# Attention first halves: softmax scaling moved from the probabilities to the product with v

## The chip, the cores and the metric

The kernel runs on one core of a Trainium2 chip as a single launch. The metric is the device time in microseconds (us). Where a profile is shown, it is one execution taken by the hardware profiler; its time axis counts from the span's start.

## The reference

Causal attention with a decay, then two feed-forward blocks. Shapes: 4 batches, 8 heads, 576 positions, head size 64; the rows of all batches form a 2304 x 512 matrix x. All in float32.

```
scores = q k^T / sqrt(D)
scores = where(causal, -1e9, scores + cum[i] - cum[j])      # cum: running sum of log f
attn   = exp(scores - rowmax)
attn   = attn / (rowsum(attn) + 1e-9)
x      = attn v                          # -> (B*S, H*D) = (2304, 512)
h = x w_in;  g = max(0.01 h, h);  x = g w_out               # first block, 512 -> 2048 -> 512
h = x w_in2; g = h * sigmoid(h);  out = g w_out2            # second block
```

## The kernel before

**Order of the work.** Each batch's 576 queries are cut in a first half (queries 0 to 255, which see 256 keys) and a second half (queries 256 to 575, which see up to 576 keys). The 64 pieces of work "head n" run in the order: n = 0 to 31 are the 8 heads of the first halves of batches 0 to 3, n = 32 to 63 those of the second halves. Two neighbouring heads make a pair, so the first halves are 16 pairs. The product x w_in of the first block (`hidden_part`, L992, tiles `hps` and `hpw`) starts as soon as the columns of x of batch 0's first half and the weights are there, and from then on it is TensorE's other work beside the attention, up to the stage where the attention has ended; the rest of the two blocks follows.

**The planner.** No engine's order is written by hand. `Plan` runs the program's generators at build time on planned costs (`act_cost`, `dve_cost`, `pe_cost` and constants in the code); each `op(engine, cost, fn, rank)` joins its engine's queue, and a lower rank goes first. Attention operations have rank 0, hidden products and the decoding of the weights rank 1. The order in which the plan issues them is the order of the instructions on each engine, and that order is fixed: an instruction that has to wait holds up all that stand behind it on its engine. A step's successor joins a queue a little after the step's planned end (`lat`), and an engine that is free at that moment takes the next operation that is ready. Until the first hidden unit is through, TensorE gets filler products (L477, L479) whenever its planned queue is empty.

**One head of a first half.** It has two blocks of 128 queries: block 0 sees 128 keys, block 1 sees 256.

1. `score`: TensorE makes the scores of a block (L775, tile `sps`), VectorE adds the mask, scales by -1/8 and takes the row minimum (L755, tile `sc`, minimum in a column of the small tile `st`), ScalarE takes the exponential and the row sums (L798).
2. `shares`: when both blocks have their exponentials, VectorE adds 1e-9 to the two sums (L817) and takes their reciprocals (L818).
3. Each block is multiplied in place by its reciprocals, on VectorE (L806) or ScalarE (L808), whichever the plan finds sooner done.
4. `transp`: TensorE transposes the three 128 x 128 pieces (L856, tile `tps`), and one copy brings them to SBUF (L372 on ScalarE or L373 on VectorE, tile `pf`).
5. `weigh`, once for a pair: TensorE multiplies v with the transposed probabilities (L925, tile `av`): the first head's 64 rows of the result go to partitions 0 to 63, the second head's to 64 to 127. Per head these are a product over 256 columns and one over 128.
6. `to_ring`: the result is split in a rounded high part (ScalarE, L372, tile `ring`) and a rest (VectorE, L387), from which the hidden product reads.

The second halves go the same way with three blocks per head. The tile `av` has one buffer (the pairs of batch 0 take turns with a second bank).

**Other work on ScalarE and VectorE in this stretch.** The weights come as 64-bit words and are decoded (L1777 on ScalarE, L1778, L1779, L1781 on VectorE, tiles `cy`, `ct`), then split (`w<-ct`, L372 and L387). A hidden product waits for the split weights it reads.

Of the kernel before, what the change touches and what calls it, by code (L numbers as in the profile page):

```python
# [9 lines left out]
F32 = mybir.dt.float32  # L10
# [3 lines left out]
ALU = mybir.AluOpType  # L14
# [6 lines left out]
G_BUFS = 3  # L21
GT_BUFS = 3
RING_BUFS = 8
WST_BUFS = 2
OUT_AT = 40
WY_BUFS = 3
# [75 lines left out]
class Plan:  # L102
# [90 lines left out]
    def wait(self, *names):  # L193
        def step(resume):
            missing = [n for n in names if n not in self.seen]
            if not missing:
                resume()
                return
            left = [len(missing)]

            def one():
                left[0] -= 1
                if not left[0]:
                    resume()

            for n in missing:
                self.waiting.setdefault(n, []).append(one)

        return step
# [8 lines left out]
    def signal(self, name):  # L218
        self.seen[name] = True
        for fn in self.waiting.pop(name, []):  # L220
            fn()

    def take(self, pool, bufs):


        def step(resume):
            i = self.taken[pool] = self.taken.get(pool, -1) + 1
            if i < bufs or (pool, i - bufs) in self.given:
                resume(i)
            else:  # L230
                self.queue[pool, i - bufs] = lambda: resume(i)

        return step

    def give(self, pool, i):
        self.given[pool, i] = True
        fn = self.queue.pop((pool, i), None)
        if fn:
            fn()
# [61 lines left out]
def fused_kernel(ctx, tc, qt, kt, va, vb, ft, w1, wi2, wo2, out):  # L301
# [430 lines left out]
    def score(n, i):  # L732
        half = head_info(n)[1]
        t0 = HALF[half][0]
        q0, qn, qk, kn = BLOCKS[half][i]
        kn = min(kn, q0 + qn)
        ht = heads[n]
        if half == 0 and i == 1:
            sc = ht["sc"][:, 256:512]
        else:  # L740
            ht["i_sc", i] = yield take("sc", SC_BUFS)
            ht["sc"] = sc = at["sc"].tile([128, S], F32, tag="sc", name="sc")
        if i == 0:
            ht["i_st"] = yield take("st", ST_BUFS)
            p.start(shares(n, stats[ht["i_st"] % ST_BUFS]))
        st = stats[ht["i_st"] % ST_BUFS]
        pieces = [(0, kn)] if kn <= 512 else [(0, kn // 2), (kn // 2, kn // 2)]
        done = []

        def least(a, ps, k0, w, bank):  # L750
            z0 = ZOFF - q0 + k0
            yield wait("zmask" if half else "zmask0")
            if a:
                yield wait(("min", n, i, a - 1))
            yield dve(w, lambda: nc.vector.tensor_tensor_reduce(  # L755
                out=sc[0:qn, k0:k0 + w], in0=ps[0:qn], in1=zmask[0:qn, z0:z0 + w], scale=-0.125,
                scalar=(MASK if a == 0 else st[0:qn, 2 * i + a - 1:2 * i + a]), op0=ALU.add, op1=ALU.min,
                accum_out=st[0:qn, 2 * i + a:2 * i + a + 1],
            ), 0)
            give(*bank)  # L760
            signal(("min", n, i, a))

        def product(ps, k0, w):
            qs = slice(q0 - t0, q0 - t0 + qn)
            if n < DIRECT:
                nc.tensor.matmul(ps[0:qn], ht["s1"][0:64, qs], ht["m1"][0:64, k0:k0 + w], start=True, stop=False)
                for c in range(w // 128):
                    nc.tensor.matmul(
                        ps[0:qn, 128 * c:w], opened["fs"][:, c, n:n + 1].broadcast_to([128, qn]),
                        opened["tri"][:, 0:w - 128 * c], start=False, stop=c == w // 128 - 1,  # L770
                    )
                return
            ops = (("s1", "m1"),) if plain(n) else (("s1", "m1"), ("s2", "m2"))
            for r, (x, y) in enumerate(ops):
                nc.tensor.matmul(  # L775
                    ps[0:qn], ht[x][:, qs], ht[y][:, k0:k0 + w], start=r == 0, stop=r == len(ops) - 1
                )

        for a, (k0, w) in enumerate(pieces):
            if n < H:  # L780
                bank = ("h", (yield take("h", 2)))
                ps = ps_h.tile([128, w], F32, tag="h", name="sps")
            else:
                bank = ("sp", (yield take("sp", 3)))
                ps = ps_at.tile([128, w], F32, tag="sp", name="sps")
            if n < DIRECT:
                yield wait("tri", ("logs", 0))
            cost = pe_cost(w, 4 if plain(n) else 2)
            if n < DIRECT:
                cost += sum(pe_cost(w - 128 * c, 4) for c in range(w // 128))  # L790
            yield op("pe", cost, lambda: product(ps, k0, w), 0, 0.05)
            p.start(least(a, ps, k0, w, bank))
        signal(("scored", n, i))
        if "i_qk" in ht and i == len(BLOCKS[half]) - 1:
            give("qk", ht["i_qk"])
        a = len(pieces) - 1
        yield wait(("min", n, i, a))
        yield act(kn, lambda: nc.scalar.activation(  # L798
            sc[0:qn, 0:kn], sc[0:qn, 0:kn], ACTF.Exp, scale=-1.0, bias=st[0:qn, 2 * i + a:2 * i + a + 1],
            accum_out=st[0:qn, 6 + i:7 + i],  # L800
        ), 0, 0.28)
        signal(("exp", n, i))
        yield wait(("shares", n))
        r = st[0:qn, 9 + i:10 + i]
        yield p.either([
            ("dve", dve_cost(kn, True) + 0.06, lambda: nc.vector.tensor_scalar(  # L806
                sc[0:qn, 0:kn], sc[0:qn, 0:kn], r, None, op0=ALU.mult), 0.0),
            ("act", act_cost(kn, 0.1), lambda: nc.scalar.mul(sc[0:qn, 0:kn], sc[0:qn, 0:kn], r), 0.0),  # L808
        ], 0, PE_LAT)
        ht["p"][i] = sc  # L810
        signal(("p", n, i))

    def shares(n, st):

        nb = len(BLOCKS[head_info(n)[1]])
        yield wait(*[("exp", n, i) for i in range(nb)])
        yield dve(1, lambda: nc.vector.tensor_scalar(st[:, 6:6 + nb], st[:, 6:6 + nb], 1e-9, None, op0=ALU.add), 0)  # L817
        yield dve(1, lambda: nc.vector.reciprocal(st[:, 9:9 + nb], st[:, 6:6 + nb]), 0)  # L818
        signal(("shares", n))
        yield wait(*[("p", n, i) for i in range(nb)])  # L820
        give("st", heads[n]["i_st"])

    def chunk_cols(half, c):

# [52 lines left out]
            p.start(rest(*w))  # L877

    def bank_for(n, tn):
        if n < H:  # L880
            name = ("av", ("acc", 0))[n // 2 % 2]
            i_av = yield take(name, 1)
            tag, pool_ = (("av", ps_at), ("acc0", ps_acc))[n // 2 % 2]
            return name, i_av, pool_.tile([128, tn], F32, tag=tag, name="av", bufs=1)
        i_av = yield take("av", 1)
        return "av", i_av, ps_at.tile([128, tn], F32, tag="av", name="av", bufs=1)
# [19 lines left out]
    def weigh(n):  # L906

        if n % 2 == 0:
            return
        _, half, _ = head_info(n)  # L910
        tn = HALF[half][1]
        both = [heads[n - 1], heads[n]]
        last = len(EDGES[half]) - 2
        chunks = range(last + 1)
        yield wait(("values", n // 2), *[("pt", m, c) for m in (n - 1, n) for c in chunks])
        v2, i_vh = pair_v.pop(n // 2)
        name, i_av, ps = yield from bank_for(n, tn)
        todo = [(c, [ht["pt"].pop(c) for ht in both]) for c in chunks]

        def product():  # L920
            for c, pts in todo:
                kw = EDGES[half][c + 1] - EDGES[half][c]
                _, lo = chunk_cols(half, c)
                for i, (pt, o, _) in enumerate(pts):
                    nc.tensor.matmul(  # L925
                        ps[64 * i:64 * i + 64, lo:tn], v2[0:kw, i, c], pt[0:kw, o:o + tn - lo],
                        start=c == 0, stop=c == last, skip_group_check=True,
                    )

        yield op("pe", 0.25 + sum(pe_cost(tn - chunk_cols(half, c)[1], 4) for c in chunks), product, 0, 0.05)  # L930
        for _, pts in todo:
            for _, _, i_pt in pts:
                for i in i_pt:
                    give("pt", i)
        if i_vh is not None:
            give("vh", i_vh)
        heads.pop(n - 1)
        heads.pop(n)
        yield from to_ring(n, ps, "a", "d")
        give(name, i_av)  # L940

    def x_ready(j, c=None):

# [1155 lines left out]
```

## Time and profile before

| | us |
|---|---|
| median of 3 runs | 946.62 (945.66 to 947.48) |
| profiled execution, its own time | 942.98 |
| its span | 941.3 |
| TensorE busy | 928.3 (99%) |
| VectorE busy | 749.0 (80%) |
| ScalarE busy | 597.9 (64%) |
| DMA | 208 GB/s mean |

Busy time counts an engine's instructions from their start to their end; TensorE's records overlap, since a product starts to stream before the one ahead has drained, so what one instruction costs is read from start to start. PE is TensorE's matmul row, PEld its weight loads, DVE is VectorE, ACT is ScalarE.

### The profile page before, as it was taken

The numbers are of one execution on the slowest core, as the hardware profiler recorded it, in microseconds if no ns is written. First come the engines' busy times: TensorE is split into PE (matmuls) and PEld (weight loads), VectorE is DVE, ScalarE is ACT, GpSimd is POOL, SyncE is SP. The second block draws the span as 40 slices with busy tenths as digits, with TensorE's granted clock in tenths as the row PEclk, the third lists the DMA queues.
The fourth block names the chain that finished last, engine by engine and source line by source line (L and its number), as shares of the span: only waits on it lengthen the run. The fifth ranks groups of instructions, "written<-read, shape, count | busy, mean of one in ns | idle before, by whom it ended". The sixth has DMA issues, their size and how long they took to land.

```text
span 941.3 us, 17621 instructions
## 1 busy us (share of the span) xinstructions
PE 928.3 (99%) x6287; PEld 877.3 (93%) x6287; DVE 749.0 (80%) x1769; ACT 597.9 (64%) x1320; POOL 54.5 (6%) x61
## 2 busy tenths in 40 slices
PE   9999999999999999999999999999999999999998
PEld 7888887788889989999999999999999999999998
DVE  6999966998998754889998699759554598888886
ACT  6899866676787763676545577556466764444442
POOL 2004302021121200000000000000000000000000
PEclk9999999999999999999999999999999999999999
DMA  7569344776676419995957685897747774544542
GB/s 201 152 176 308 120 128 152 250 235 226 217 250 189 141 57 314 347 363 181 326 214 234 170 266 171 290 336 251 271 169 245 238 239 116 154 116 139 147 120 90
DMA packets 157523, 195.42 MB, mean 208 GB/s; under 512 B 9222, under 2 KB 142966, under 8 KB 157404
## 3 DMA queue, kind: packets, MB, share of 16 engines
q1 hardware_dynamic: 157004, 193.91, 64.1%
q8 instruction: 49, 0.80, 0.4%
q10 hardware_dynamic: 432, 0.39, 0.1%
q14 instruction: 38, 0.31, 0.1%
HBM read 124.61 MB, written 69.65 MB: 206 GB/s over the span
## 4 chain that ended last, share of the span: by engine, by line
PE 71%; DVE 11%; DMA 10%; ACT 5%; issue 2%; SPq 1%; DVEq 0%; ACTq 0%
PE m L1590 19%; PE m L1732 18%; PE hpw L992 11%; PE acc L1283 8%; PE sps L775 4%; PE av L925 4%; PE tps L856 3%; DMA w<-w_d 3%; DMA g_d<-gw 2%; DMA gq<-g_d 2%; DVE sc L755 2%; PE hps L992 2%; DVE gs L387 2%; ACT sc L798 1%; DMA w_d<-f 1%
## 5 line engine op out<-in xcount | busy, mean ns | idle before, releaser
L1283 PE MATMUL acc<-gs,w 128*128 128x384 f32 x1008 | 181.5, 339 | 1.2 <-DVE gs L387 1.0
L992 PE MATMUL hpw<-ring,w 128*128 128x320 f32 (+1 forms) x960 | 179.7, 330 | 0.2 <-ACT gw L1104 0.2
L1590 PE MATMUL m<-xc,w 128*128 128x384 f32 x1008 | 179.8, 339 | 0.0
L1283 PEld LDWEIGHTS acc<-gs,w 128*128 128x128 f32 x1008 | 177.6, 188 | 2.2 <-DVE gs L387 1.6
L1732 PE MATMUL m<-w,gc 128*128 128x256 f32 x1512 | 178.6, 280 | 0.0
L1732 PEld LDWEIGHTS m<-w,gc 128*128 128x128 f32 x1512 | 178.4, 188 | 0.0
L1590 PEld LDWEIGHTS m<-xc,w 128*128 128x128 f32 x1008 | 177.7, 188 | 0.2
L992 PEld LDWEIGHTS hpw<-ring,w 128*128 128x128 f32 x960 | 149.8, 188 | 7.0 <-issue 0.5
L372 ACT CAST gc<-g 128x512 fp32r<-128x512 f32 (+1 forms) x180 | 80.4, 490 | 88.7 <-DVE g L1422 50.6
L798 ACT ACTIVATE sc<-sc,st 128x576 f32<-128x576 f32 (+2 forms) x160 | 93.0, 582 | 30.6 <-DVE st L755 29.1
L1216 ACT CAST gs<-gq 128x768 fp32r<-128x768 f32 x84 | 69.6, 835 | 47.5 <-PE acc L1283 26.1
L387 DVE TENSOR_TENSOR gs<-gq,gs 128x768 fp32r<-128x768 f32 x84 | 79.5, 952 | 18.0 <-ACT gs L1216 17.5
L387 DVE TENSOR_TENSOR gc<-g,gc 128x512 fp32r<-128x512 f32 (+1 forms) x180 | 89.8, 524 | 3.3 <-ACT gc L372 2.1
L755 DVE CUSTOM_DVE_ANT_0 sc<-sps,zmask 128x288 f32<-128x288 f32 (+2 forms) x160 | 71.4, 449 | 24.6 <-PE sps L775 16.0
L1422 DVE TENSOR_TENSOR g<-g 128x256 f32<-128x256 f32 x144 | 58.3, 418 | 18.6 <-DMA g<-g_d 18.0
L856 PE MATMUL tps<-ident,sc 66*107 66x66 f32 (+3 forms) x480 | 67.4, 269 | 1.4 <-DVE st L755 0.4
L775 PE MATMUL sps<-m,s 66*128 66x288 f32 (+5 forms) x256 | 64.1, 331 | 4.4 <-DVE st L755 2.7
L387 DVE TENSOR_TENSOR w<-w 128x512 fp32r<-128x512 f32 x84 | 56.0, 686 | 15.1 <-ACT w L1984 15.1
L1984 ACT CAST w<-w 128x512 fp32r<-128x512 f32 x84 | 50.9, 619 | 24.1 <-DMA w<-w_d 23.7
L383 POOL TENSOR_TENSOR m<-qk,m 64x288 fp32r<-64x288 f32 x46 | 49.4, 1095 | 266.5 <-ACT m L372 127.9
L856 PEld LDWEIGHTS tps<-ident,sc 66*107 66x107 f32 (+3 forms) x480 | 55.8, 151 | 7.1 <-issue 1.2
L992 PE MATMUL hps<-ring,w 128*128 128x256 f32 x384 | 58.7, 291 | 0.0
(125 smaller groups left out, 1129.1 us busy)
## 6 DMA issues: line engine op xcount, KB each, us to landing
w<-w_d SPq DMA_DIRECT2D x84, 256.0 KB
gq<-g_d SPq DMA_DIRECT2D x48, 384.0 KB
g_d<-z SPq DMA_DIRECT2D x24, 768.0 KB
g<-g_d SPq DMA_DIRECT2D x36, 512.0 KB
w_d<-f SPq DMA_DIRECT2D x16, 896.0 KB
g_d<-gw SPq DMA_DIRECT2D x32, 320.0 KB
qk<-in_kt_dram SPq DMA_DIRECT2D x32, 288.0 KB
wst<-in_w_dram SPq DMA_DIRECT2D x18, 512.0 KB
```

The lines of the kernel that those rows point to most:

```text
L372: ("act", act_cost(n, base), lambda: nc.scalar.copy(dst, src), 0.0),
L387: ("dve", dve_cost(n), lambda: nc.vector.tensor_tensor(dst, a, b, op=ALU.subtract), 0.0),
L755: yield dve(w, lambda: nc.vector.tensor_tensor_reduce(out=sc[0:qn, k0:k0 + w], in0=ps[0:qn], in1=zmask[0:qn, z0:z0 + w], scale=-0.125, sca ...
L775: nc.tensor.matmul(ps[0:qn], ht[x][:, qs], ht[y][:, k0:k0 + w], start=r == 0, stop=r == len(ops) - 1)
L798: yield act(kn, lambda: nc.scalar.activation(sc[0:qn, 0:kn], sc[0:qn, 0:kn], ACTF.Exp, scale=-1.0, bias=st[0:qn, 2 * i + a:2 * i + a + 1], ...
L856: nc.tensor.transpose(ps[0:k1 - k0, o:o + qn], ht["p"][i][0:qn, k0:k1], ident[0:qn, 0:qn])
L992: nc.tensor.matmul(dst, w[:, wi, c * 128:(c + 1) * 128], x(xi, c), start=(first_ and c == 0 and r == 0), stop=(c == KC - 1 and r == 2), sk ...
L1216: yield act(2 * TB, lambda: nc.scalar.copy(t[:, 0], src), 0, 0.09)
L1283: nc.tensor.matmul(dst, w[:, e, wi, j * 128:(j + 1) * 128], x[:, xi, e], start=start and s == 0 and e == 0 and r == 0, stop=stop and s == ...
L1422: ("dve", dve_cost(n), lambda: nc.vector.tensor_tensor(dst, a, b, op=op_), 0.0),
L1590: nc.tensor.matmul(dst, w[:, wi, c * 128:(c + 1) * 128], x[:, xi, c], start=start and c == 0 and r == 0, stop=stop and c == 1 and r == 2, ...
L1732: nc.tensor.matmul(banks[b][:, e], t[:, gi, a * 128:(a + 1) * 128], w[:, wi], start=begin and a == 0 and r == 0, stop=jp == NP // 2 - 1 an ...
```

## The change

It concerns the first halves alone (n = 0 to 31). Step 3 is dropped: the exponentials go to the transposes and to the product with v as they are. The small tile `st` is now shared by a pair: minima in columns 0 to 3, sums in 4 to 7, reciprocals in 8 to 11; step 2 runs once per pair (`pair_shares`), on four columns.

In `weigh` the pair's bank grows from 256 to 512 columns. Ahead of the product with v TensorE makes four products into the upper 256 columns (`spread`): for each block and each head a reciprocal column, repeated 64 times, is the 128 x 64 weight, and the 128 x 128 identity is streamed. The result holds, in the 64 partitions of each head, the reciprocal of each query in its column. One copy (`factors`, on ScalarE or VectorE) brings these 256 columns to SBUF, in a new tile `xn` with two buffers; after the product with v, VectorE multiplies the product by them into the same tile, which frees the bank, and `to_ring` reads `xn` instead of the bank.

```
         signal(("exp", n, i))
+        if not half:
+            yield p.after(PE_LAT - LAT)
+            ht["p"][i] = sc
+            signal(("p", n, i))
+            return
         yield wait(("shares", n))
...
+    def pair_shares(n, st):
+        yield wait(*[("exp", m, i) for m in (n, n + 1) for i in range(2)])
+        yield dve(1, lambda: nc.vector.tensor_scalar(st[:, 4:8], st[:, 4:8], 1e-9, None, op0=ALU.add), 0)
+        yield op("dve", dve_cost(1), lambda: nc.vector.reciprocal(st[:, 8:12], st[:, 4:8]), 0, PE_LAT)
+        signal(("shares", n))
...
     def bank_for(n, tn):
+        if head_info(n)[1] == 0:
+            tn = 2 * tn
...
-        yield wait(("values", n // 2), *[("pt", m, c) for m in (n - 1, n) for c in chunks])
+        yield wait(("values", n // 2), *([] if half else [("shares", n - 1)]), *[("pt", m, c) for m in (n - 1, n) for c in chunks])
...
+        def spread():
+            for i, (q0, qn, _, _) in enumerate(BLOCKS[0]):
+                for e in range(2):
+                    r = st[:, 8 + 2 * i + e:9 + 2 * i + e].broadcast_to([128, D])
+                    nc.tensor.matmul(
+                        ps[64 * e:64 * e + 64, tn + q0:tn + q0 + qn], r, ident, start=True, stop=True,
+                        skip_group_check=True,
+                    )
+        def factors():
+            yield copy(tn, x, ps[:, tn:2 * tn], "ad", 0, None, 0.125, False)
+        if not half:
+            i_x = yield take("xn", XN_BUFS)
+            x = at["const"].tile([128, tn], F32, tag="xn", name="xn", bufs=XN_BUFS)
+            yield op("pe", 0.5, spread, 0, 0.05)
+            give("st", i_st)
+            p.start(factors(), lambda: signal(("factors", n)))
...
-        yield from to_ring(n, ps, "a", "d")
+        if half:
+            yield from to_ring(n, ps, "a", "d")
+            give(name, i_av)
+            return
+        yield wait(("factors", n))
+        yield op("dve", 0.42, lambda: nc.vector.tensor_tensor(x, ps[:, 0:tn], x, op=ALU.mult), 0)
         give(name, i_av)
+        yield from to_ring(n, x, "a", "d")
+        give("xn", i_x)
```

## Rows read from the trace of the kernel before

**Rows 1.** Busy us (instructions) of PE, PEld, DVE, ACT, POOL by stretch; granted clock; DMA.

```profile
12.00:33.00 21.00, 21.00 (x167) 18.07 (x165) 20.33 (x97) 18.36 (x62) 0.00 (x0) 1.00 0.68 183
33.00:80.00 47.00, 46.62 (x360) 38.85 (x359) 46.10 (x198) 44.01 (x144) 2.72 (x2) 1.00 0.69 203
80.00:120.00 40.00, 36.70 (x287) 33.03 (x286) 39.36 (x105) 35.10 (x83) 16.41 (x14) 1.00 0.54 172
120.00:941.30 821.30, 812.82 (x5433) 778.87 (x5432) 639.89 (x1352) 494.74 (x1021) 30.31 (x30) 1.00 0.65 211
```

**Rows 2.** Timeline, TensorE, 32 to 38 us: start, duration, instruction and count.

```profile
32.77 0.60 PE L775 MATMUL sps<-k,s 65*128 65x256 f32 x2
33.20 0.49 PE L856 MATMUL tps<-ident,sc 128*128 128x128 f32 x3
33.62 0.87 PE L925 MATMUL av<-pf,v 128*64 128x256 f32 x8
...
34.67 0.60 PE L992 MATMUL hps<-ring,w 128*128 128x256 f32 x3
...
37.69 0.87 PE L925 MATMUL av<-pf,v 128*64 128x256 f32 x8
```

**Rows 3.** Groups by form, TensorE, 33 to 80 us: busy, mean ns, idle before.

```profile
L992 PE MATMUL hps<-ring,w 128*128 128x256 f32 x132 | 23.5, 305 | 0.0
```

**Rows 4.** Timeline, TensorE's dense stretch: 60 hidden records and the next start.

```profile
127.19 7.36 PE L992 MATMUL hps<-ring,w 128*128 128x256 f32 x60
134.39 2.23 PE L992 MATMUL hpw<-ring,w 128*128 128x512 f32 x9
```

**Rows 5.** Waits of TensorE, 80 to 120 us: us in total, times, longest.

```profile
PE sps L775 <- DVE st L755: 1.4, 2, 0.8
```

**Rows 6.** Timeline, TensorE around one pair's product with v.

```profile
59.33 0.60 PE L775 MATMUL sps<-k,s 65*128 65x256 f32 x2
59.85 0.87 PE L925 MATMUL av<-pf,v 128*64 128x256 f32 x8
60.65 0.49 PE L775 MATMUL sps<-k,s 65*128 65x128 f32 x2
```

**Rows 7.** Timeline, TensorE's weight loads around the same product (idle before, releaser).

```profile
59.85 0.63 PEld L925 LDWEIGHTS av<-pf,v 128*64 128x64 f32 x8 [0.33 <-issue]
60.65 0.30 PEld L775 LDWEIGHTS sps<-k,s 65*128 65x128 f32 x2 [0.17 <-DVE st L818]
```

**Rows 8.** Groups by form, 0 to 95 us: fillers, scalings, the shares' two steps.

```profile
L479 PE MATMUL fps<-zmask 128*128 128x128 f32 x60 | 10.3, 274 | 0.0
...
L806 DVE TENSOR_SCALAR sc<-sc,st 128x256 f32<-128x256 f32 x23 | 8.0, 346 | 0.0
...
L808 ACT ACTIVATE sc<-sc,st 128x128 f32<-128x128 f32 x14 | 5.5, 393 | 0.2 <-DVE st L818 0.2
L817 DVE TENSOR_SCALAR st<-st 128x2 f32<-128x2 f32 x32 | 5.2, 162 | 0.6 <-ACT sc L798 0.5
L818 DVE RECIPROCAL st<-st 128x2 f32<-128x2 f32 x32 | 5.1, 158 | 0.0
L806 DVE TENSOR_SCALAR sc<-sc,st 128x128 f32<-128x128 f32 x18 | 5.0, 280 | 0.0
...
L808 ACT ACTIVATE sc<-sc,st 128x256 f32<-128x256 f32 x9 | 4.5, 499 | 0.0
```

**Rows 9.** Timeline, VectorE, 30 to 33 us.

```profile
30.44 0.16 DVE L818 RECIPROCAL st<-st 128x2 f32<-128x2 f32 x1
30.52 0.40 DVE L387 TENSOR_TENSOR ring<-av,ring 128x256 fp32r<-128x256 f32 x1
...
30.84 0.54 DVE L806 TENSOR_SCALAR sc<-sc,st 128x128 f32<-128x128 f32 x2
...
31.29 0.16 DVE L817 TENSOR_SCALAR st<-st 128x2 f32<-128x2 f32 x1
...
32.51 0.69 DVE L387 TENSOR_TENSOR w<-ct,w 128x512 fp32r<-128x512 f32 x1
```

More of the change, by code (lines that the diff above doesn't have):

```diff
@@ L23 @@
 RING_BUFS = 8
+XN_BUFS = 2
 WST_BUFS = 2
@@ L743, in score @@
         if i == 0:
-            ht["i_st"] = yield take("st", ST_BUFS)
-            p.start(shares(n, stats[ht["i_st"] % ST_BUFS]))
+            if half or n % 2 == 0:
+                ht["i_st"] = yield take("st", ST_BUFS)
+                p.start((shares if half else pair_shares)(n, stats[ht["i_st"] % ST_BUFS]))
+            else:
+                ht["i_st"] = heads[n - 1]["i_st"]
         st = stats[ht["i_st"] % ST_BUFS]
+        col = (lambda a: 2 * i + a) if half else (lambda a: 2 * i + n % 2)
+        total = 6 + i if half else 4 + 2 * i + n % 2
         pieces = [(0, kn)] if kn <= 512 else [(0, kn // 2), (kn // 2, kn // 2)]
@@ L756, in least @@
                 out=sc[0:qn, k0:k0 + w], in0=ps[0:qn], in1=zmask[0:qn, z0:z0 + w], scale=-0.125,
-                scalar=(MASK if a == 0 else st[0:qn, 2 * i + a - 1:2 * i + a]), op0=ALU.add, op1=ALU.min,
-                accum_out=st[0:qn, 2 * i + a:2 * i + a + 1],
+                scalar=(MASK if a == 0 else st[0:qn, col(a - 1):col(a - 1) + 1]), op0=ALU.add, op1=ALU.min,
+                accum_out=st[0:qn, col(a):col(a) + 1],
             ), 0)
@@ L798, in score @@
         yield act(kn, lambda: nc.scalar.activation(
-            sc[0:qn, 0:kn], sc[0:qn, 0:kn], ACTF.Exp, scale=-1.0, bias=st[0:qn, 2 * i + a:2 * i + a + 1],
-            accum_out=st[0:qn, 6 + i:7 + i],
+            sc[0:qn, 0:kn], sc[0:qn, 0:kn], ACTF.Exp, scale=-1.0, bias=st[0:qn, col(a):col(a) + 1],
+            accum_out=st[0:qn, total:total + 1],
         ), 0, 0.28)
         signal(("exp", n, i))
+        if not half:
[3 more added lines that the diff above has]
+            return
         yield wait(("shares", n))
@@ L918, in weigh @@
         todo = [(c, [ht["pt"].pop(c) for ht in both]) for c in chunks]
+        i_st = both[0].get("i_st")
+        st = stats[i_st % ST_BUFS]
+        def spread():
[14 more added lines that the diff above has]
+            p.start(factors(), lambda: signal(("factors", n)))
         def product():
@@ L928, in product @@
                     )
-        yield op("pe", 0.25 + sum(pe_cost(tn - chunk_cols(half, c)[1], 4) for c in chunks), product, 0, 0.05)
+        yield op("pe", 0.25 + sum(pe_cost(tn - chunk_cols(half, c)[1], 4) for c in chunks),
+                 product, 0, 0.05)
         for _, pts in todo:
```

## The prediction

> **What bounds the kernel now.** I read the busy times by stretch first. The reader is to see that TensorE is at work all the time at a granted clock of 1.00 (2.4 GHz): it is idle for 0.4 us between 33 and 80, for 3.3 us between 80 and 120, and for 8.5 us in the 821 us behind that [rows 1]. In the two stretches from 12 to 80 VectorE is busy 97 and 98%, ScalarE 87 and 94%; from 120 on they have room (78 and 60%) [rows 1]. The first halves, which the change touches, begin in the first of these stretches and end early in the third, and there three engines are full together. So the question is which of them sets the pace there.
>
> A busy TensorE can hide small gaps, so I looked at what fills it. Between 33 and 80 it does 132 records of the hidden product with no idle time ahead of them [rows 3]. In a dense stretch 60 such records take from 127.19 to 134.39, 0.12 us each [rows 4], so they are 15.8 of the 47 us, and they are work that waits for its turn: the plan never ran out of it. What the attention takes more of TensorE there pushes hidden work back by the same amount, and since TensorE is idle for no more than 8.5 us of the 821 that follow, what is pushed back comes out at the end. What the attention takes less of VectorE and ScalarE brings nothing by itself in that stretch; it can only bring something at the two places where TensorE has no real work or waits.
>
> The first place is ahead of 34.67, where the first hidden product stands [rows 2]. Up to there TensorE's gaps hold 60 filler records [rows 8]. The hidden product needs split weights; the last step of the second weight stands in VectorE's order at 32.51, for 0.69 us [rows 9]. Then a pair's product with v goes first, at 33.62 [rows 2]. So this start hangs on VectorE, which is full. The second place is 80 to 120: the 3.3 us there [rows 1] are TensorE held up in its order by late VectorE results, the largest group of them scores that wait for a row minimum [rows 5].
>
> **The change, part by part.**
>
> *TensorE, added: four small products per pair.* Nothing like `spread` stands in the trace; the product with v is nearest, since it too has 64-column weights and two heads side by side. A score product over 256 columns takes from 32.77 to 33.20, 0.43 us [rows 2], so one over 128 columns takes 0.215. The product with v is two of 256 and two of 128 columns, 1.29 us one after the other; it takes from 59.85 to 60.65, 0.80 us [rows 6], so the two heads' products run side by side (0.645) with 0.155 us lost behind them. Ahead of it the score product that began at 59.33 lasts to 59.85, 0.52 us where 0.43 is usual [rows 2, 6], 0.09 more. Going into and out of this shape thus costs 0.245 us, which the idle time ahead of the weight loads also shows [rows 7]. The four products of `spread` are 4 x 128 columns in two columns of the array: 0.43 us side by side, 0.86 if they do not overlap. If they stood directly ahead of the product with v, they would share its way in and out: 0.43. But the product with v joins the queue 0.05 us after the planned end of `spread`, and TensorE, free at that moment, takes the next hidden piece, which is always ready. So I expect them apart, each with its own 0.245: 0.43 + 0.245 = 0.68 us. Bounds: 0.43 (adjacent) to 0.86 + 0.245 = 1.1 (no overlap). I take 0.68.
>
> The Trainium skill, page "TensorEngine Tiling (Array Packing)", section Key Properties, says that changing the tiling mode, not just the tile, drains TensorE. By that rule each `spread` that stands apart pays a drain of its own, which the idle times ahead of the loads bear out [rows 7]; the sum would be the one at 0.68, not the one at 0.43.
>
> Four of the 16 pairs have their product with v ahead of 34.67 (the fifth stands at 33.62 [rows 2] and belongs to the saturated part). Those four take the place of fillers: 4 x 0.68 = 2.7 us against 60 records of about half of 0.215, 6.5 us [rows 2, 8]; they cost nothing as long as these fillers are there, and 2.7 us if they were not. The other 12 cost 12 x 0.68 = **+8.2 us** (5.2 to 13).
>
> *VectorE and ScalarE, removed.* The 64 scalings: 41 on VectorE (23 of 256 and 18 of 128 columns), 23 on ScalarE [rows 8]. One of each form on VectorE take from 30.84 to 31.29 together, 0.45 us [rows 9]; split by their durations 0.25 and 0.20, this makes 23 x 0.25 + 18 x 0.20 = 9.4 us. On ScalarE 5.5 + 4.5 = 10.0 us at full durations [rows 8], some 8 with the overlap that VectorE's have. Of the 64 steps on sums 32 go; one takes from 30.44 to 30.52, 0.08 us to the next start [rows 9], so 2.6 us.
>
> *VectorE and ScalarE, added.* 16 products with the factors, a VectorE operation of 128 x 256 from PSUM, like the rest for the ring: 30.52 to 30.84, 0.32 us [rows 9], 5.1 us. 16 copies of the factors, same size, on either engine, some 5 us. Net relief: 9.4 + 8 + 2.6 - 5.1 - 5 = about 10 us over both, 5 each, of some 70 us in which they are full.
>
> *What the relief brings.* Ahead of the start, 5 of 16 pairs' worth: 10 x 5/16 = 3.1 us over two engines, 1.5 us on each. Against it stands the longer way of the last pair of batch 0: `spread`, a piece of other work, the product with the factors, some 1 us more, and the scaling and its hand-overs, about as long, less. The weights decide rather than that pair, so I take **-1.0 us** (0 to -3). In 80 to 120, VectorE has 3 or 4 us less behind it; of the 3.3 us of idle time there, and 0.4 before [rows 1], I take 70% back: **-2.6 us** (0 to -3.7).
>
> *Waits that are added.* `spread` waits for the pair's reciprocals; behind it on TensorE stand scores and hidden pieces. Between the last exponential and the product with v lie the transposes and a copy, longer than the two steps of 0.16 us [rows 8], so I cost this at nothing; were that cover gone, each 0.1 us late would cost 12 x 0.1 = 1.2 us. The product with the factors waits for the copy of them; behind it on VectorE stand row minima and copies of transposes. The product with v and a hidden piece, together over 1 us, cover the copy. The bank is held longer, about 3 us in place of 2; pairs follow each other by 37.69 - 33.62 = 4.1 us [rows 2], so I cost that at nothing, and 0.5 us a pair, 6 us, if it did not fit. No DMA is added or moved.
>
> *The sum.* 8.2 - 1.0 - 2.6 = +4.6 us. On the profiled execution's own 942.98 (1.7 around its span of 941.3) that is 947.6; the median of the runs shown stands 3.6 us above it, at 946.62, and on that the forecast is **951.2 us**.
>
> **The rivals.**
>
> *A, TensorE has room (faster).* Its weight loads are busy for 38.85 of 47 us between 33 and 80 [rows 1], so 8.2 us are without one. If the stretch is really paced by VectorE and ScalarE, the 12 x 0.68 fit into that room, and only the gains stand: -1.0 - 2.6 = -3.6, 943.0 us. It decides if less than 1.7 us of the 8.2 shows. Against it: the hidden records have no idle time ahead of them [rows 3], and a score record of 0.215 us streams longer than its load takes, so a share below one is no proof of room. The Trainium skill, page "Perfetto Trace Analysis", section Identifying the Most-Contended Engine, holds busy matmul time for a bad measure and weight-load busy time for a good one; by that rule TensorE stands at 83% there, VectorE at 98% is the bound, and this rival is right. Chance 0.16.
>
> *B, cheap and recovered (same).* `spread` costs 0.43, 5.2 us in all, and the gains reach their ends, -3.7 and -1.0: +0.5, 947.1 us. It needs the plan to set the two products together. Chance 0.18.
>
> *C, no overlap (slower, more).* The copies of one column as weights do not run side by side: 12 x 1.1 = 13.2, less 3.6: +9.6, 956.2 us. Chance 0.09.
>
> *D, a new wait (slower).* The bank or the factors come late: 4.6 + 6, about 957 us; or the plan, which is made anew with other costs, sets other waits behind 120, where 8.5 us of idle time [rows 1] can grow as well as shrink. Chance 0.06.
>
> **How the numbers follow.** The forecast, +2 to +8.5, has 0.51. A change within 0.2%, 1.9 us, is about what a measurement of this kernel can't tell from none. Slower: 0.51 + 0.09 + 0.06 = 0.66; same: B, 0.18; faster: A, 0.16. The range goes from A's 943.0 to 956.0, just under C, so that about 2 in 10 are outside; the forecast's own is 948.6 to 955.
>
> **What would show it.** In the profile after: 128 weight loads more of 64 columns, in groups of 8 that take 0.6 to 0.7 us to the next start and stand apart from the product with v; no scaling lines at the first halves; the first hidden record at 33 to 34.5; less TensorE idle time between 80 and 120; and the same record of the second stage (the dense stretch's end, say) some 4 to 5 us later. The forecast is wrong if hidden records get through as early as before despite `spread`, if the groups take under 0.45 us or over 0.9, or if idle time behind 120 changes by more than 3 us.

## The result, and the profile after

| | before | after |
|---|---|---|
| median of 7 runs each | 946.62 us (944.66 to 948.67) | 952.65 us (949.57 to 954.80) |
| ratio after / before | | 1.0075, 95% interval 1.0056 to 1.0094 |
| profiled execution, its span | 941.3 us | 949.9 us |

By the ratio the change makes the kernel 7.1 us slower (5.3 to 8.9); the two medians differ by 6.0. I had forecast 4.6 us slower. The changed kernel, run once more beside other experiments (e8), came out at 1.0089 (1.0074 to 1.0105). The profiled execution stands 8.6 us above that of before.

First the busy times by stretch of the changed kernel, columns as in [rows 1]:

```profile
12.00:33.00 21.00, 19.16 (x153) 15.04 (x151) 16.95 (x69) 16.67 (x56) 0.00 (x0) 1.00 0.57 154
33.00:80.00 47.00, 46.78 (x378) 35.33 (x374) 44.92 (x170) 39.79 (x130) 1.56 (x2) 1.00 0.72 210
80.00:120.00 40.00, 38.96 (x305) 34.45 (x304) 38.60 (x113) 35.67 (x86) 15.07 (x14) 1.00 0.56 175
120.00:949.90 829.90, 820.83 (x5500) 786.76 (x5498) 640.70 (x1353) 497.03 (x1023) 30.55 (x31) 1.00 0.64 209
```

The relief is there: between 12 and 80 VectorE is busy for 61.9 us in place of 66.4, ScalarE for 56.5 in place of 62.4 [rows 1]. TensorE's idle time between 80 and 120 fell from 3.3 us to 1.0, nearly as forecast. But behind 120 it is 9.1 in place of 8.5, and ahead of 33 there are 1.8 us that were not there before; 1.1 of them are a score product that waits for the load of the keys of a later head (in e8, the same kernel, the idle time ahead of 33 is 0.7). All four stretches together have 12.2 us of idle time before and 12.2 after. So idle time makes none of the 8.6 us. Where they come from stands in the records of the hidden product alone, here of the changed kernel (columns: PE, PEld, granted clock, DMA):

```profile
33.00:80.00 47.00, 10.56 (x57) 7.89 (x57) 1.00 0.72 210
80.00:120.00 40.00, 22.46 (x157) 20.27 (x156) 1.00 0.56 175
```

57 records got through between 33 and 80, where there were 132 [rows 3]. Another 9 ran ahead of 33, the first at 27.3, so by 80 there are 66 fewer. At the 0.12 us of a dense stretch [rows 4] that is 7.9 us of hidden work pushed back. The forecast's sign, a record of the second stage that starts 4 to 5 us later, came out larger too: the wide hidden records (tile `hpw`) start at 142.0 in place of 134.4 [rows 4], and the last of them at 418.7 in place of 409.3 (the last two times of such a line are the group's first and last start):

```profile
L1042 PE MATMUL hpw<-ring,w x960: 302/309/496, 142.0 to 418.7; 128*128 128x320 f32 x153, 128*128 128x512 f32 x39
```

What took the place shows in TensorE's timeline of one pair in the changed kernel:

```profile
38.61 0.60 PE L781 MATMUL sps<-k,s 65*128 65x256 f32 x2
39.14 0.66 PE L947 MATMUL av<-ident,st 128*64 128x128 f32 x8
39.73 0.49 PE L781 MATMUL sps<-k,s 65*128 65x128 f32 x2
40.05 0.49 PE L874 MATMUL tps<-ident,sc 128*128 128x128 f32 x3
40.48 0.87 PE L967 MATMUL av<-pf,v 128*64 128x256 f32 x8
41.28 0.70 PE L781 MATMUL sps<-k,s 65*128 65x256 f32 x2
```

The small products (L947) stand apart from the product with v (L967), as forecast. They take from 39.14 to 39.73, 0.59 us, the 0.43 side by side and 0.155 behind them that the working had. The score product ahead takes 0.53 us where 0.43 is usual, about the 0.09 of the way in that the working had as well. But the score product behind them also takes longer, from 39.73 to 40.05, 0.32 us, where the working had 0.215 for one of 128 columns: another 0.10, which the forecast did not count. The rows of before have it as well, behind a product with v:

```profile
60.65 0.49 PE L775 MATMUL sps<-k,s 65*128 65x128 f32 x2
60.90 0.60 PE L992 MATMUL hps<-ring,w 128*128 128x256 f32 x3
...
36.58 0.39 PE L775 MATMUL sps<-k,s 65*128 65x128 f32 x2
36.72 0.60 PE L992 MATMUL hps<-ring,w 128*128 128x256 f32 x3
```

The first score product stands right behind a product with v and takes 0.25 us to the next start, the second stands elsewhere and takes 0.14.

The groups by form of the changed kernel, 0 to 95 us (columns as in [rows 3]), show the rest:

```profile
L947 PE MATMUL av<-ident,st 128*64 128x128 f32 x128 | 10.5, 285 | 0.0
...
L987 DVE TENSOR_TENSOR xn<-av,xn 128x256 f32<-128x256 f32 x16 | 6.6, 410 | 0.5 <-ACT xn L373 0.5
...
L374 DVE COPY xn<-av 128x256 f32<-128x256 f32 x13 | 5.5, 425 | 2.7 <-PE av L967 2.1 <-PE av L947 0.5
L480 PE MATMUL fps<-zmask 128*128 128x128 f32 x24 | 4.2, 278 | 0.0
...
L373 ACT COPY xn<-av 128x256 f32<-128x256 f32 x3 | 1.1, 373 | 1.2 <-PE av L967 0.8 <-PE av L947 0.2
```

All 128 records of the small products; 13 of the 16 copies on VectorE, 3 on ScalarE; and 24 fillers where there were 60 [rows 8].

### The profile page after: what moved, and what is told of

Same layout as the page of the kernel before. It is cut to its first block, busy times and chain, and to the rows that moved or that the text cites. A ratio compares the mean times of both kernels' runs of the same rounds, so it can differ in the third digit from the quotient of the medians.

```text
span 949.9 us, 17741 instructions
## 1 busy us (share of the span) xinstructions
PE 936.9 (99%) x6379; PEld 880.3 (93%) x6379; DVE 744.5 (78%) x1721; ACT 594.8 (63%) x1304; POOL 52.2 (5%) x61
## 4 chain that ended last, share of the span: by engine, by line
PE 77%; DVE 10%; DMA 6%; ACT 3%; issue 2%; SPq 1%; DVEq 0%; ACTq 0%
PE m L1640 19%; PE m L1782 18%; PE hpw L1042 11%; PE acc L1333 11%; PE sps L781 5%; PE av L967 5%; PE tps L874 4%; PE hps L1042 3%; DVE gs L388 2%; DVE sc L761 1%; DMA gq<-g_d 1%; DMA qk<-in_kt_dram 1%; DMA w_d<-wf 1%; PE av L947 1%; DMA g_d<-gw 1%
## 5 line engine op out<-in xcount | busy, mean ns | idle before, releaser
L384 POOL TENSOR_TENSOR m<-qk,m 64x288 fp32r<-64x288 f32 x46 | 47.2, 1046 | 277.3 <-ACT m L373 96.5
L1042 PE MATMUL hps<-ring,w 128*128 128x256 f32 x384 | 55.8, 289 | 0.0
```

Source lines behind the costliest of these rows:

```text
L1042: nc.tensor.matmul(dst, w[:, wi, c * 128:(c + 1) * 128], x(xi, c), start=(first_ and c == 0 and r == 0), stop=(c == KC - 1 and r == 2), sk ...
```

## The experiments

Theory 1 is the forecast's: TensorE is full, and what is added to it pushes hidden work back. Theory 2: the loss is the longer way to the ring (the copy of the factors, the product with them on VectorE, and their waits). Theory 3: VectorE and ScalarE set the pace of the first halves. Differences in us are the ratio times the median of before in the same job.

| run | what it is | ratio to before (95%) | us |
|---|---|---|---|
| e1 | before + small products | 1.0129 (1.0100 to 1.0159) | +12.2 |
| e2 | relief alone | 0.9987 (0.9973 to 1.0002) | -1.2 |
| e3, e10 | small products and product with v in one operation | 1.0073 (1.0049 to 1.0098), 1.0054 (1.0039 to 1.0070) | +6.9, +5.1 |
| e4 | change for batch 0 alone | 1.0006 (0.9990 to 1.0021) | +0.6 |
| e5 | before + longer way to the ring | 1.0105 (1.0086 to 1.0124) | +9.9 |
| e6 | change, small products twice | 1.0209 (1.0194 to 1.0224) | +19.8 |
| e7 | as e3, small products in bfloat16 | 0.9973 (0.9951 to 0.9995) | -2.6 |
| e8 | change again | 1.0089 (1.0074 to 1.0105) | +8.4 |
| e9 | as e3, reciprocals in two bfloat16 parts | 1.0038 (1.0022 to 1.0055) | +3.6 |
| e11 | e7, another plan | 0.9979 (0.9961 to 0.9996) | -2.0 |
| e12 | before, another plan | 1.0024 (1.0013 to 1.0034) | +2.3 |

**e1, the small products alone.**

```
     def bank_for(n, tn):
+        if head_info(n)[1] == 0:
+            tn = 2 * tn
...
+                        ps[64 * e:64 * e + 64, tn + q0:tn + q0 + qn], ident[:, 0:1].broadcast_to([128, D]), ident,
...
+        if not half:
+            yield op("pe", 0.5, spread, 0, 0.05)
```

> The kernel before, with the four small products per pair added and nothing else: they read a constant column as weights and nobody reads their result; scalings, shares and ring stay as before, so the output is unchanged. Theory 1 (TensorE is full, what is added there pushes hidden work back): +8 to +10 us on before, 12 pairs at 0.68 to 0.8 us, since no relief of VectorE gives anything back. Theory 2 (the change's loss comes from the longer way to the ring, with its copy, its product on VectorE and its waits): below +2 us. Hidden records between 33 and 80 us: by theory 1 some 70 fewer than before's 132, by theory 2 no fewer than 120.

Measured +12.2 us (9.4 to 15.0). Hidden records of this kernel between 33 and 80:

```profile
33.00:80.00 47.00, 14.63 (x81) 11.04 (x81) 1.00 0.67 195
```

81 in place of 132, and 6 more ahead of 33: 45 fewer by 80, 5.4 us at 0.12. VectorE and ScalarE have the same operations as before, the way to the ring is the old one. So the small products alone cost at least as much as the whole change, which theory 2 can't make. Not all of the 12.2 us is TensorE's time for them, though. In the profiled execution, 11.3 us above before's span, TensorE idles 9.1 us from 120 to 930 where it idled 4.5: the plan is made anew and has other waits there. And two of the six runs, at 959.6 and 962.0 us, have a mean granted clock of 0.996; the other four, at 1.000, lie 9 to 11 us above the median of before.

**e2, the relief alone.**

```
-            i_x = yield take("xn", XN_BUFS)
-            x = at["const"].tile([128, tn], F32, tag="xn", name="xn", bufs=XN_BUFS)
-            yield op("pe", 0.5, spread, 0, 0.05)
             give("st", i_st)
-            p.start(factors(), lambda: signal(("factors", n)))
...
-        if half:
-            yield from to_ring(n, ps, "a", "d")
...
+        yield from to_ring(n, ps, "a", "d")
         give(name, i_av)
```

> The changed kernel without the small products, the copy of the factors and the product with them: the first halves are left unnormalized, so the output is not the reference's. It is the relief of VectorE and ScalarE alone, about 20 us over both (no scalings, half of the steps on sums, nothing added). Theory 1: it can only bring idle and filler time back, -3 to -5 us on before. Theory 3 (VectorE and ScalarE set the pace of the first halves): half of the relief or more, -8 to -10 us.

Measured -1.2 us (-2.5 to +0.2). Some 20 us of work less on VectorE and ScalarE, in stretches where they were up to 98% busy, are worth next to nothing: theory 3 falls as stated, and theory 1's -3 to -5 was too much as well. Fillers fell from 60 to 32, but TensorE now idles 3.1 us between 33 and 80, where it idled 0.4 [rows 1]; the largest wait, 1.3 us, is that of a product with v for VectorE, which is then at the split of a weight. In its trace the last narrow hidden record (tile `hps`) and the last wide one (`hpw`) start at (last time of each line):

```profile
L1029 PE MATMUL hpw<-ring,w x960: 302/309/496, 132.1 to 409.5; 128*128 128x320 f32 x153, 128*128 128x512 f32 x39
...
L1029 PE MATMUL hps<-ring,w x384: 276/283/472, 24.4 to 132.0; 128*128 128x256 f32 x192
```

and in the kernel before:

```profile
L992 PE MATMUL hpw<-ring,w x960: 302/309/496, 134.4 to 409.3; 128*128 128x320 f32 x153, 128*128 128x512 f32 x39
...
L992 PE MATMUL hps<-ring,w x384: 277/283/472, 34.7 to 134.3; 128*128 128x256 f32 x192
```

The relief starts the hidden product 10 us earlier and has its narrow part done 2.3 us earlier; at the end of the wide part, 0.2 us later, nothing is left of it.

**e3 and e10, one way in and out less.**

```
+            yield op("pe", 0.43 + 0.25 + sum(pe_cost(tn - chunk_cols(half, c)[1], 4) for c in chunks),
+                     lambda: (spread(), product()), 0, 0.05)
```

> The changed kernel with the small products and the product with v issued as one TensorE operation, so that no other work comes between them. Theory 1: one way into and out of the 64-column shape less per pair, 12 x 0.245 = 2.9 us off the changed kernel, so +3 to +5 us on before. Theory 2: the factors come later, behind the product, so the product with them waits longer: no better than the changed kernel, +6 to +9 us.

> The kernel of e3 once more, since its runs lay in two groups (about 949 and 956 us). Theory 1, from e8 and the trace of e3 (hidden records between 33 and 88 us: 112 against 81 in the changed kernel): +4.5 to +6 us on before, 3 us under the changed kernel. Theory 2: as the changed kernel, +7 to +9 us.

TensorE's timeline of one pair in e3:

```profile
45.34 0.66 PE L947 MATMUL av<-ident,st 128*64 128x128 f32 x8
45.83 0.82 PE L964 MATMUL av<-pf,v 128*64 128x256 f32 x8
46.58 0.70 PE L781 MATMUL sps<-k,s 65*128 65x256 f32 x2
```

Together 1.24 us; apart they took 0.59 and 0.80, with two ways in. Hidden records between 33 and 80 of e3:

```profile
33.00:80.00 47.00, 16.79 (x96) 13.12 (x96) 1.00 0.67 185
```

96 in place of the change's 57, and 19 ahead of 33 in place of 9. In e10's profiled execution, the same kernel, it is 81 (and 21 ahead), at a mean granted clock of 0.93 in the stretch. The time followed less clearly: e3's runs lay in two groups, seven from 946.6 to 950.3 and three from 955.3 to 956.5 us, and its mean was no better than the change's; e10's six runs gave +5.1 (3.7 to 6.6), against +8.4 (7.0 to 9.9) of e8 in another job. That agrees with the 2.9 us expected. The upper group of e3 was not traced; its mean granted clock is 0.994 to 0.996, that of the lower group 0.996 to 1.000.

**e4, the change for batch 0 alone** (a condition `n < H` in place of `not half`).

> The change for the first halves of batch 0 alone (n below 8); batches 1 to 3 as before. Theory 1: the four pairs' small products take the place of fillers and cost nothing, and the hidden product starts up to 1 us earlier: 0 to -1.5 us on before. Theory 2: a quarter of the change's loss of some 7 us: +1.5 to +2 us.

Measured +0.6 us (-0.9 to +2.0). The interval reaches into the ranges of both theories, so the time doesn't settle whether the first four pairs' small products are free or are just paid for by the relief.

**e5, the longer way to the ring alone.**

```
+        def factors():
+            yield wait("zmask")
+            yield copy(tn, x, zmask[:, 0:tn], "ad", 0, None, 0.125, False)
...
+        yield op("dve", 0.42, lambda: nc.vector.tensor_tensor(x, ps[:, 0:tn], x, op=ALU.add), 0)
         give(name, i_av)
+        yield from to_ring(n, x, "a", "d")
```

> The kernel before (probabilities scaled as before, no small products), with the longer way to the ring alone: per pair of the first halves a copy of 256 zero columns into the new tile, an addition of it to the product with v on VectorE, and the ring reading the tile. The output is unchanged. Some 10 us of work more for VectorE and ScalarE, none for TensorE. Theory 1 (TensorE's time is the loss): 0 to +2 us on before. Theory 2 (the longer way and its waits are the loss): +4 to +7 us.

Measured +9.9 us (8.1 to 11.7): theory 1's 0 to +2 is wrong, and it is more than theory 2's +4 to +7. Its copy reads zeros, so the wait for the small products is not in it. That some 10 us more for VectorE and ScalarE cost some 10 us does not mean that they come out one for one. The profiled execution, the fastest of the five at a span of 947.1 (5.8 above before), has lost nothing up to 120. Hidden records of e5, then of before:

```profile
33.00:80.00 47.00, 22.15 (x126) 17.12 (x126) 1.00 0.63 182
80.00:120.00 40.00, 24.17 (x162) 21.43 (x162) 1.00 0.68 209
...
33.00:80.00 47.00, 23.55 (x132) 18.04 (x132) 1.00 0.69 203
80.00:120.00 40.00, 22.48 (x156) 20.68 (x156) 1.00 0.54 172
```

288 in both, with none ahead of 33. Most of the loss is in one place behind that. All busy times of e5 in steps of 5 us:

```profile
125.00:130.00 5.00, 4.33 (x34) 4.13 (x34) 5.00 (x14) 4.56 (x11) 3.35 (x1) 1.00 0.31 103
130.00:135.00 5.00, 2.18 (x11) 1.98 (x12) 3.13 (x5) 2.10 (x4) 5.00 (x4) 0.86 0.32 108
135.00:140.00 5.00, 5.00 (x36) 5.00 (x36) 0.00 (x0) 0.05 (x1) 0.46 (x1) 0.80 0.00 0
140.00:145.00 5.00, 5.00 (x34) 3.30 (x34) 1.06 (x3) 1.43 (x4) 0.00 (x0) 1.00 0.32 107
```

and one row of its timeline:

```profile
132.21 0.50 PE L1008 MATMUL hps<-ring,w 128*128 128x256 f32 x2 [2.30 <-ACT w L373]
```

The hidden product waits for a weight that ScalarE has yet to round. The weights are decoded at a lower rank than the attention; that the added attention work has delayed the decoding up to here is likely, but no run tests it. Between 130 and 135 TensorE idles 2.8 us, and in the stretches from 130 to 140 the mean granted clock is 0.86 and 0.80, which is another 1.7 us of its work: 4.5 of the 5.8 us. The other four runs, 3.4 to 7.8 us slower, were not traced; their mean granted clock is 0.994 to 0.996 against 0.998 here. So this loss is of another kind than the change's, whose runs have 0.999 to 1.000.

**e6, the small products twice.**

```
             yield op("pe", 0.5, spread, 0, 0.05)
+            yield op("pe", 0.5, spread, 0, 0.05)
```

> The changed kernel with the four small products made twice per pair, as two TensorE operations, the second writing the same values over the first. Theory 1: 12 x 0.68 = 8 us more again, +14 to +17 us on before. Theory 2: no worse than the changed kernel, +6 to +9 us.

Measured +19.8 us (18.3 to 21.2), 11.4 more than e8 in the same job: 0.71 us for each of 16 pairs. Fillers are 22, in e8 24, so no filler pays for the second set. Hidden records between 33 and 80 of e6:

```profile
33.00:80.00 47.00, 3.71 (x18) 2.60 (x18) 1.00 0.57 167
```

18, and 6 ahead of 33. The theories' bounds were 14 to 17 and 6 to 9; it is theory 1's side, and dearer than theory 1 had it.

**e7, the small products in bfloat16.** One record for each product in place of two.

```
+    ident_r = at["const"].tile([128, 128], mybir.dt.bfloat16, name="ident_r")
...
+    st_rs = [const.tile([128, 4], mybir.dt.bfloat16, name=f"sr{i}") for i in range(ST_BUFS)]
...
+        yield op("dve", dve_cost(1), lambda: nc.vector.tensor_copy(st_r, st[:, 8:12]), 0, PE_LAT)
```

> The kernel of e3 (small products and product with v in one TensorE operation) with the small products in bfloat16: one record per product in place of two and one pass; the reciprocals are rounded to bfloat16, so the output is less exact. One small VectorE operation more per pair, and one buffer for the new tile in place of two. Everything else of the change stays. Theory 1: the small products cost 0.1 to 0.2 us a pair, 1 to 2.5 us, less e2's relief of 1.2: 0 to +1.5 us on before. Theory 2: the way to the ring is as long as before: +5 to +8 us.

Measured -2.6 us (-4.6 to -0.5), slightly faster than before. In its trace the small products take 0.14 us and stand directly ahead of the product with v:

```profile
38.35 0.30 PE L953 MATMUL av<-ident_r,sr 128*64 128x128 bf16 x4
38.49 0.82 PE L970 MATMUL av<-pf,v 128*64 128x256 f32 x8
```

The way to the ring is as long as in the change, and the loss is gone. So theory 2 falls here: with the scalings dropped, the longer way is paid for.

**e8, the change again.**

> The changed kernel itself once more, on the chip of e5 to e7, to set beside them: +5.5 to +9 us on before by both theories.

**e9, two bfloat16 parts.** Each reciprocal is kept as a rounded part and a rest, and two products add them up.

```
+        parts = st[:, 0:4].bitcast(BF16)
...
+        yield dve(1, lambda: nc.vector.tensor_copy(parts[:, 0:4], st[:, 8:12]), 0)
+        yield op("dve", dve_cost(1), lambda: nc.vector.tensor_tensor(
+            parts[:, 4:8], st[:, 8:12], parts[:, 0:4], op=ALU.subtract), 0, PE_LAT)
...
+                    for a in range(2):
...
+                            st[:, 0:4].bitcast(BF16)[:, k:k + 1].broadcast_to([128, D]), ident.bitcast(BF16)[:, 1::2],
```

> The kernel of e3 (small products and product with v in one TensorE operation), with each reciprocal split into two bfloat16 parts (the first rounded, the second the rest, also rounded), which two single-pass products add up in the bank; the identity is the upper half of each float32 word of the identity that is there. Two small VectorE operations more per pair than in the changed kernel, two buffers for the new tile. Theory 1: the small products cost about 0.25 us a pair, 0.12 more than in e7, some 2 us in all: -2 to +1 us on before. Theory 2: +5 to +8 us.

Measured +3.6 us (2.1 to 5.2), between what the two theories expected. Its small products take 0.26 us a pair, as expected (45.42 to 45.68 in one pair), so 2 us more than e7; the 6 us between them are not explained by TensorE's time alone. That raised the question what a new plan is worth by itself.

**e11 and e12, other plans for the same work** (the planned cost of one operation 0.1 us higher).

> The kernel of e7 with one number changed: the planned cost of the product with v and its small products is 0.1 us higher, so the plan sets the same instructions in another order. The work is the same. If the order that a new plan happens to make is worth little, it is within 1.5 us of e7 (-4 to -1 us on before); if such orders are worth some us, as e9 suggests (6 us behind e7 with 2 us more work), it may lie anywhere from -4 to +4 us.

> The kernel before with the planned cost of the product with v 0.1 us higher: the same instructions in another order. If orders are worth little: within 1 us of before. If they are worth some us: up to 4 us to either side.

e11 stays with e7 (-2.0, -3.7 to -0.4). e12, with not an instruction more than before, is 2.3 us slower (1.2 to 3.2). So an order that a plan happens to make can be worth some 2 us, and sums of this study are not finer than that. Only these two orders were tried.

## Why the prediction was right, and where not

**The side and the cause were right.** TensorE is full in the first halves, the hidden product waits for its turn, and what the small products take is missing in hidden records: by 80 there are 132, 66 and 24 of them with none, one and two sets of small products, and adding the products alone costs +12.2 us (e1).

TensorE's whole span can be added up by kind, each instruction counted from its start to the next start, idle time apart. Against before, the profiled execution of the change has 9.5 us more of small products, 2.7 more of score products and 1.6 more of transposes, 0.8 less of hidden product, 3.7 less of fillers and 0.7 less of the rest. Its idle time is the same within 0.1. These sum to the 8.6 us. (e2 has 1.4 us more of transposes without any small products, so that part does not come from them.)

**The price of the small products was too low.** I had 0.68 us a pair. The rows of the changed kernel give 0.59 for the products, 0.10 for the operation ahead and another 0.10 for the one behind, 0.79 in all; the last term is the one that I had left out. A second set (e6 against e8) agrees: 9.4 us more of small products and 3.3 more of score products, 0.79 for each of 16 pairs, and +11.4 us in the times. Between e7's cheap products and e8's lie 11.0.

**The fillers paid what I had them pay.** I let four pairs go free, 2.7 us, and took 1.0 us for the earlier start. Both come out of the fillers, which fell from 60 to 24, by the 3.7 us above. It is not the small products of these pairs alone that replaced them: the relief alone leaves 32 (e2), the small products alone 40 (e1).

**The idle time did not come back.** Here the forecast's term failed by most: I took 2.6 us back. 2.3 came back between 80 and 120 and 0.2 ahead of that, but 1.8 are new ahead of 33 and 0.6 behind 120. In e8's profiled execution, the same kernel, 1.2 us came back in all. So the sum should have been 16 times 0.79, less 3.7, less nothing: 8.9 in place of 4.6.

The Trainium skill (page "TensorEngine Tiling (Array Packing)", section Key Properties) states that a change of tiling mode drains TensorE. The trace agrees: the two groups of 64-column products take 0.59 and 0.80 us apart, and 1.24 together (e3), where one way in and out less is paid.

**What VectorE and ScalarE are worth is only half answered.** 20 us less on them brought 1.2 us (e2), so they did not set the pace. But 10 us more cost 9.9 (e5), through a stall behind the first halves and a lower clock, and the slower runs of e5 were not traced. How much can be added there before it costs stays open.

**Rival A fell.** TensorE had no room for the small products (e1), and the relief alone is worth next to nothing (e2). The rule on weight-load busy time (the Trainium skill, page "Perfetto Trace Analysis", section Identifying the Most-Contended Engine) would have had VectorE as the bound there. e1 and e2 are against it, and in e5's trace 10 us of added work for VectorE and ScalarE pushed back no hidden record by 120. **Rival B** had the right price for products set directly together: 1.24 less 0.80, 0.44 us a pair. But the plan did not set them so, and where they are set so (e3, e10) the kernel is still 5 to 7 us slower, and the recovery that B counted on did not happen. **Rival C** fell: the two heads' products run side by side, 0.59 us. **Rival D**: no wait of TensorE for the bank or the factors shows. Other waits behind 120 made 0.6 us in the change, but 4.6 in e1.

**What comes out ahead of both kernels** is e7 and e11, by 2 to 2.6 us, at the price of reciprocals rounded to bfloat16. That is about as much as another order alone moved (e12).

## What to carry to other kernels

Where low-ranked work fills every gap of an engine, count how many of its records get through a stretch: that shows what an addition costs when busy time stays at 99%. Add up the engine's time by kind from start to next start, so that the longer times of the neighbours are counted and not only those of the added work. Moving work from one full engine to another full one is paid at the price of the receiver, and the giver's relief may be worth next to nothing: idle time that it takes away in one stretch can come back in another. So measure the relief alone and the addition alone. When small products must be added, make them cheap (here by a type with half the records) and put them next to products of the same shape, and test a kernel with a planned order against a replanned copy of itself before reading a difference of 0.2%.

## What the runs showed of the hardware

A short idle time costs more than itself through the clock. In e7's profiled execution, one of its slower ones, ScalarE waited in its order for words of weights:

```profile
55.28 0.66 ACT L1836 ACTIVATE cy<-wsg 128x512 f32<-128x512 f32 x1 [2.53 <-DMA wsg<-in_w_dram]
```

VectorE and TensorE ran dry behind it, and then the granted clock fell below its upper level (2.4 GHz) in the next stretch (busy times of e7):

```profile
53.00:58.00 5.00, 3.41 (x25) 2.17 (x24) 2.57 (x12) 2.72 (x10) 0.00 (x0) 0.95 0.70 196
58.00:63.00 5.00, 5.00 (x34) 4.30 (x33) 4.37 (x20) 4.32 (x15) 0.00 (x0) 0.71 0.42 125
```

A mean clock of 0.71 and 0.95 over two stretches of 5 us is 1.7 us of TensorE's work lost, about as much as the 1.6 us of idle time ahead. e5 has the same behind its stall, 1.7 us lost by the clock behind 2.8 us of idle time. e7's twelve runs lie in two groups, seven from 938.5 to 941.6 and five from 944.0 to 948.7 us. The mean granted clock of the seven is 0.998 to 1.000, that of four of the five 0.994 to 0.996; the fifth is this one, 0.998. That such waits make the difference is likely, but only this one execution was traced.
